# One weight load of the last feed-forward stage issued as fifteen loads of a few partitions each

## The chip, the cores and the metric

The kernel runs on one core of one Trainium2 chip. The metric is the device time of one execution in microseconds (us). Before the change it is 711.88 us, the median of three runs.

## The reference

Four tokens (B = 4, one per sequence) pass through an attention block and a feed-forward block, and then through both again with the same weights:

```python
x = A_x
x = x + _A_ref(_layernorm(x), A_k_cache, A_v_cache, A_wq, A_wo)   # 32 heads of 128, window 1024
x = x + _B_ref(_layernorm(x), B_w1, B_w2)                         # relu(x @ w1) @ w2
x = x + _A_ref(_layernorm(x), A_k_cache, A_v_cache, A_wq, A_wo)
x = x + _B_ref(_layernorm(x), B_w1, B_w2)
```

x is [4, 1, 640], w1 is [640, 1728], w2 is [1728, 640], all in float32. Per head the kernel needs a part of wq, the last 1024 keys and values of four sequences, and a part of wo. A head does not stay on the chip from the first round to the second, except for the last few.

## The kernel before

The host packs all that one head needs into one record of 9,472 float32 columns on 128 partitions (`rec`): wq, keys, values, wo. It packs w1 and w2 into a second array, `w`: first five pieces of 1,728 columns for w1 (one for each k, a fifth of the 640 inputs), then 54 tiles of 160 columns for w2. Two buffers on the chip take the loads: `slots`, five places of one record each, and `ring`, one place of 9,152 columns which the feed-forward stages use too.

The order of all loads is a list, `items`, written at the start. `pump()` takes loads from the head of the list and issues them on one queue, that of SyncE (SP), as long as the columns that a load will overwrite are free; `done()` and `free()` mark columns as free after the last use has been written down, and call `pump()`. Everything in that queue is issued in the order of the list, one instruction after the other, and an instruction that waits holds up all behind it.

The scheduling layer gives the loads eight completion semaphores in turn, DMAHW0 to DMAHW7. A load may not be issued before the load that used the same semaphore, eight loads earlier, has landed. So no more than eight loads are under way at a time, whatever their size.

The work around the change is the end of round two. After the record loads come the loads of the last feed-forward stage. The w1 loads are four, since the first two pieces travel together: 3,456 columns (k = 0 and 1), then 1,728 columns three times (k = 2, 3 and 4), all into `ring`. The w2 loads are five: 3,520, 2,240, 1,600, 640 and 640 columns, into a place of `slots`. On TensorE (PE), `mlp()` uses them in this order: 20 products with w1 in `h_ps`, relu and transposes, then products with the w2 tiles added into `acc`. Then VectorE copies the result to `scratch`, and SP issues the store of `out`. The constants `W1_SLOT` and `W2_SLOT` give the cuts of these loads.

Nearly all instructions are recorded by the helper `InOrder`, so the profile gives them its line 94 in the kernel before.

Of the kernel before, what the change touches and what calls it, by code (L numbers as in the profile page):

```python
# [2 lines left out]

# [11 lines left out]
P = 128  # L40
B, D, H, DH, W, FF = 4, 640, 32, 128, 1024, 1728
# [33 lines left out]
W1_SLOT = [[0, 1], [2], [3], [4]]  # L75
W2_SLOT = [22, 14, 10, 4, 4]
LATE = 5


class InOrder:  # L80
# [21 lines left out]
def decode_kernel(ctx: ExitStack, tc: tile.TileContext, xf, rec, w, out):  # L102
    nc = tc.nc
    pe, dve, act, pool, sp = (InOrder(tc, e) for e in (nc.tensor, nc.vector, nc.scalar, nc.gpsimd, nc.sync))
# [11 lines left out]
    hT = scratch.rearrange("p (m j) -> p m j", j=32)  # L116
    oTs = sb.tile([P, LATE, B], F32, name="oTs")
    qT = sb.tile([P, B], F32, name="qT")
# [59 lines left out]
    buffers = {"slots": slots, "ring": ring}  # L178
# [8 lines left out]
    def piece(r, h, lo, hi, buf=None, col=None):  # L187
        buf, col = place(home(h, r) if buf is None else buf, lo if col is None else col)
        items.append(([(("rec", r, h), lo, hi, col)], rec, h * REC + lo, h * REC + hi, buf, col))
# [9 lines left out]
    def ending(r, hs, late):  # L199
# [4 lines left out]
        if late:  # L204
            for h in hs[-1:] + hs[-LATE:-1]:
                piece(r, h, WO, REC)
# [8 lines left out]
    for h in hs[5 * NS:-3]:  # L215
        piece(0, h, 0, RING if h == SIXTH else WO if h >= H - LATE else REC)
    piece(0, SIXTH, RING, REC, "ring", 0)
    ending(0, hs, True)
    n = 0
# [22 lines left out]
    n = W1_COLS  # L242
# [4 lines left out]
    def pump():  # L247

        while items:
            parts, src, lo, hi, buf, col = items[0]  # L250
            if any(b == buf and x < col + hi - lo and col < y for b, x, y in live):
                return
            sp.dma_start(buffers[buf][:, col:col + hi - lo], src[:, lo:hi])
            live.append((buf, col, col + hi - lo))
            for key, x, y, c in parts:
                at.setdefault(key, []).append((x, y, buf, c))
            items.pop(0)
# [20 lines left out]
    def done(key, lo, hi):  # L278

        if key[0] == "rec" and key[1] == 0 and key[2] >= LAST:  # L280
            return
        if key == ("rec", 0, SIXTH):
            hi = min(hi, HELD)
        for x, y, buf, col in pieces(key):
            a, b = col + max(lo, x) - x, col + min(hi, y) - x
            if a < b:
                free(buf, a, b)
        pump()
# [5 lines left out]
    def put_by():  # L294

        for col, a, b in held:
            dve.tensor_copy(hold[:, col:col + b - a], ring[:, a:b])
            free("ring", a, b)
        free("ring", BESIDE, KEPT)
        pump()  # L300

    def lend():

        act.activation(*lent, AF.Copy)
        free("ring", HELD, BESIDE)
        pump()
# [193 lines left out]
    for r in range(2):  # L500
        hs = order[r]
        late = LATE if r == 0 else 2
        if r == 0:
# [92 lines left out]
```

## Time and profile before

| What | Value |
|---|---|
| device time, median of 3 runs | 711.88 us (711.86 to 713.6) |
| profiled execution | span 710.5 us from its first to its last instruction; its device time is not given beside it, and 711.88 less 710.5 leaves 1.4 us around a span |
| DMA | busy share 0.9 or more in 39 of 40 slices; mean 426 GB/s; 302.64 MB |
| PE busy | 513.6 us, 72% of the span |
| VectorE (DVE) busy | 323.3 us, 46% |
| ScalarE (ACT) busy | 99.7 us, 14% |

The profile gives an issue of a load as an instruction of SPq (about 0.33 us); the transfer itself goes on afterwards in 16 DMA engines, and its end is the landing. The views of windows give the busy share of those 16 engines in a stretch of time (the overlap of packets can bring it a little over 1.00) and the bytes moved.

### The profile page before, as it was taken

To read this page: it belongs to the slowest core of one execution; us is meant where nothing else is said; L and a number is where in the kernel's file an instruction comes from. 1 tells how busy PE (TensorE), PEld (TensorE's weight loads), DVE (VectorE), ACT (ScalarE), POOL (GpSimd) and SP (SyncE) were. 2 spreads that over 40 slices of the span, in tenths; PEclk is the share of its full clock that TensorE was granted. 3 is DMA by queue.
4 is the path that set the end of the run, shared out by engine and by line. 5 is a ranking of instruction groups with operands and counts; after the bars stand their busy time and mean duration, and the time that the engine had idled before them with its cause. 6 is when DMAs were issued, how large, how long until landed. Compare 5 with 4: busy or idle time off the path is not lost.

```text
span 710.5 us, 8690 instructions
## 1 busy us (share of the span) xinstructions
PE 513.6 (72%) x3706; PEld 202.8 (29%) x3706; DVE 323.3 (46%) x678; ACT 99.7 (14%) x211; POOL 1.1 (0%) x9
## 2 busy tenths in 40 slices
PE   3567686678584578857888898865686677576897
PEld 2132232232231223322223334331331322231423
DVE  3333353353452353546641777644352444253762
ACT  1100110011010110111121212201010111011111
POOL 0000000000000000000000000000000000000000
PEclk9957787677777776888999899977576677677899
DMA  9999999999999999999999999999999999999997
GB/s 381 463 409 451 415 442 443 414 442 444 424 429 440 434 429 421 435 425 430 424 416 403 421 435 428 438 434 448 429 445 427 428 442 430 427 442 406 431 423 292
DMA packets 13318, 302.64 MB, mean 426 GB/s; under 512 B 1488, under 2 KB 1760, under 8 KB 5216
## 3 DMA queue, kind: packets, MB, share of 16 engines
q1 hardware_dynamic: 13248, 302.08, 99.1%
q8 instruction: 29, 0.48, 0.2%
q14 instruction: 9, 0.07, 0.0%
q10 hardware_dynamic: 32, 0.01, 0.0%
HBM read 302.00 MB, written 0.08 MB: 425 GB/s over the span
## 4 chain that ended last, share of the span: by engine, by line
DMA 73%; PE 21%; DVE 4%; issue 1%; ACT 1%; SPq 0%; ACTq 0%; DVEq 0%
DMA slots<-rec 57%; PE sc_ps L94 11%; DMA ring<-w 8%; PE o_ps L94 7%; DMA ring<-rec 5%; PE acc L94 2%; DMA slots<-w 2%; DVE scratch L94 2%; DVE o_ps L94 1%; ACT oTs L94 1%; DVE small L94 0%; ACT sc_ps L94 0%; DVE turned L94 0%; SPq L94 0%; DVE ring L94 0%
## 5 line engine op out<-in xcount | busy, mean ns | idle before, releaser
L94 PE MATMUL sc_ps<-slots,qT 128*4 128x512 f32 x992 | 194.5, 869 | 37.4 <-DMA slots<-rec 36.4
L94 PE MATMUL sc_ps<-xT,slots 128*128 128x4 f32 x620 | 94.6, 279 | 99.8 <-DMA slots<-rec 99.2
L94 PE MATMUL o_ps<-slots,scratch 128*16 128x512 f32 x960 | 149.3, 693 | 2.4 <-DVE scratch L94 1.7
L94 DVE TENSOR_REDUCE small<-sc_ps 128x1 f32<-128x1024 f32 x64 | 78.3, 1224 | 156.9 <-PE sc_ps L94 156.9
L94 PEld LDWEIGHTS sc_ps<-xT,slots 128*128 128x128 f32 x620 | 89.2, 225 | 157.8 <-DMA slots<-rec 109.0
L94 ACT ACTIVATE sc_ps<-sc_ps,small 128x1024 f32<-128x1024 f32 (+1 forms) x68 | 71.1, 1046 | 342.2 <-DVE small L94 340.7
L94 DVE STREAM_TRANSPOSE turned<-sc_ps 128x1024 f32<-128x1024 f32 (+1 forms) x85 | 84.6, 996 | 0.7
L94 PEld LDWEIGHTS o_ps<-slots,scratch 128*16 128x16 f32 x960 | 34.5, 118 | 120.0 <-issue 107.6
L94 DVE TENSOR_TENSOR o_ps<-o_ps,of_block 128x512 f32<-128x512 f32 x62 | 43.4, 699 | 53.6 <-PE o_ps L94 52.3
L94 PEld LDWEIGHTS sc_ps<-slots,qT 128*4 128x4 f32 x992 | 32.3, 108 | 121.9 <-issue 64.9
L94 DVE TENSOR_TENSOR qT<-sc_ps,by_row 128x4 f32<-128x4 f32 x62 | 9.7, 156 | 114.1 <-PE sc_ps L94 114.1
L94 PE MATMUL acc<-slots,oTs 128*4 128x160 f32 x496 | 35.4, 368 | 19.2 <-ACT oTs L94 18.5
L94 DVE TENSOR_REDUCE scratch<-o_ps 128x128 f32<-128x512 f32 x62 | 42.9, 691 | 2.1
L94 ACT ACTIVATE oTs<-o_ps 128x4 f32<-128x4 f32 x64 | 11.1, 174 | 214.1 <-PE o_ps L94 214.1
L94 PE MATMUL o_ps<-pick,scratch 128*128 128x4 f32 x128 | 26.8, 280 | 15.9 <-DVE scratch L94 15.9
L94 PEld LDWEIGHTS o_ps<-pick,scratch 128*128 128x128 f32 x128 | 22.4, 218 | 21.4 <-DVE scratch L94 21.1
L94 DVE TENSOR_TENSOR scratch<-turned,by_row 128x128 f32<-128x128 f32 (+1 forms) x85 | 22.0, 259 | 3.2
L94 PE MATMUL sc_ps<-slots,small 128*1 128x512 f32 (+2 forms) x56 | 21.5, 486 | 0.0
L94 DVE TENSOR_SCALAR by_row<-of_batch,small 128x4 f32<-128x4 f32 x64 | 14.7, 230 | 2.2
L94 PEld LDWEIGHTS acc<-slots,oTs 128*4 128x4 f32 x496 | 6.9, 84 | 25.2 <-ACT oTs L94 23.5
L94 DVE STREAM_TRANSPOSE scratch<-small 128x32 f32<-128x32 f32 x64 | 12.9, 202 | 2.2 <-ACT sc_ps L94 2.2
L94 ACT ACTIVATION_READ_ACCUMULATOR sc_ps<-sc_ps,small 128x1 f32 x64 | 12.3, 193 | 0.0
(66 smaller groups left out, 103.7 us busy)
## 6 DMA issues: line engine op xcount, KB each, us to landing
slots<-rec SPq DMA_DIRECT2D x15, 7872.0 KB, 27.0
slots<-rec SPq DMA_DIRECT2D x8, 7936.0 KB, 31.5
slots<-rec SPq DMA_DIRECT2D x17, 2368.0 KB, 16.9
slots<-rec SPq DMA_DIRECT2D x4, 4736.0 KB, 25.9
slots<-rec SPq DMA_DIRECT2D x2, 4416.0 KB, 29.3
slots<-rec SPq DMA_DIRECT2D x7, 1024.0 KB, 19.7
ring<-w SPq DMA_DIRECT2D x8, 864.0 KB, 10.9
ring<-rec SPq DMA_DIRECT2D x1, 4576.0 KB, 36.2
```

Of the source, the lines that this page charges most:

```text
L94: r = build(*args, **kwargs)
```

## The change

The third w1 piece of round two, k = 2, columns 3,456 to 5,183 of `w`, is no longer one load of 128 partitions. It comes as fifteen loads, each of a band of neighbouring partitions: 2, 3, 4, and so on up to 15, and 9 at the end, 128 in sum. Destination, data and place in the list are the same. No other engine's instructions change. (Blank lines at the file's head are gone too, so that the same code has smaller line numbers: 94 becomes 72.)

```diff
+BANDED = 2 * FF
+BANDS = [2, 3, 4, 5, 6, 7, 8, 9, 10, 11, 12, 13, 14, 15, 9]
+assert sum(BANDS) == P
...
-            sp.dma_start(buffers[buf][:, col:col + hi - lo], src[:, lo:hi])
+            a = 0
+            for n in BANDS if parts and parts[0][:2] == (("w", 1), BANDED) else (P,):
+                sp.dma_start(buffers[buf][a:a + n, col:col + hi - lo], src[a:a + n, lo:hi])
+                a += n
```

SP's instructions from the first w1 load of round two on, before the change (partitions x columns, and the semaphores waited for):

```order
L94 DMA ring<-w 128x3456 [waits DMAHW6_49,DVE_49]
L94 DMA ring<-w 128x1728 [waits DMAHW7_49]
L94 DMA ring<-w 128x1728 [waits DMAHW0_49,DVE_49,Activation_49]
L94 DMA ring<-w 128x1728 [waits DMAHW1_49]
L94 DMA slots<-w 128x3520 [waits DMAHW2_49]
L94 DMA slots<-w 128x2240 [waits DMAHW3_49,PE_49]
L94 DMA slots<-w 128x1600 [waits DMAHW4_49,PE_49]
L94 DMA slots<-w 128x640 [waits DMAHW5_49,PE_49]
L94 DMA slots<-w 128x640 [waits DMAHW6_49,PE_49]
```

The first and the last of these nine rows wait for the same semaphore: the last w2 load waits for the landing of the 3,456-column load. The seven loads between them wait for record loads issued earlier.

The same place on SP after the change, first up to the seventh band:

```order
L72 DMA ring<-w 128x3456 [waits DMAHW6_49,DVE_49]
L72 DMA ring<-w 2x1728 [waits DMAHW7_49]
L72 DMA ring<-w 3x1728 [waits DMAHW0_49]
L72 DMA ring<-w 4x1728 [waits DMAHW1_49]
L72 DMA ring<-w 5x1728 [waits DMAHW2_49]
L72 DMA ring<-w 6x1728 [waits DMAHW3_49]
L72 DMA ring<-w 7x1728 [waits DMAHW4_49]
L72 DMA ring<-w 8x1728 [waits DMAHW5_49]
```

The seven waits for record loads are now those of the first seven bands.

And SP's next twelve instructions:

```order
L72 DMA ring<-w 9x1728 [waits DMAHW6_49]
L72 DMA ring<-w 10x1728 [waits DMAHW7_49]
L72 DMA ring<-w 11x1728 [waits DMAHW0_49]
L72 DMA ring<-w 12x1728 [waits DMAHW1_49]
L72 DMA ring<-w 13x1728 [waits DMAHW2_49]
L72 DMA ring<-w 14x1728 [waits DMAHW3_49]
L72 DMA ring<-w 15x1728 [waits DMAHW4_49]
L72 DMA ring<-w 9x1728 [waits DMAHW5_49]
L72 DMA ring<-w 128x1728 [waits DMAHW6_49,DVE_49,Activation_49]
L72 DMA ring<-w 128x1728 [waits DMAHW7_49]
L72 DMA slots<-w 128x3520 [waits DMAHW0_49]
L72 DMA slots<-w 128x2240 [waits DMAHW1_49,PE_49]
```

The eighth band (9 partitions) now has the wait for the 3,456-column load, which the last w2 load had; the fourth and fifth w1 pieces and all w2 loads stand behind it.

## The prediction

> **What bounds the kernel now.** I read the page first: the engines' shares, the slices, the chain that ended last. Then the chain in order of time, for the end of round two alone, since the change is there.
>
> ```profile
> span 710.5 us, 8690 instructions
> PE 513.6 (72%) x3706; PEld 202.8 (29%) x3706; DVE 323.3 (46%) x678; ACT 99.7 (14%) x211; POOL 1.1 (0%) x9
> DMA  9999999999999999999999999999999999999997
> DMA 73%; PE 21%; DVE 4%; issue 1%; ACT 1%; SPq 0%; ACTq 0%; DVEq 0%
> ...
> 660.59 0.33 SPq L94
> 661.02 29.53 DMA ring<-w
> 690.61 16.54 DMA slots<-w
> 707.19 0.50 PE acc L94 x8
> ```
>
> PE is busy 72% of the span, the DMA engines nine tenths or more in all slices but the last, and 73% of the chain is transfers. The chain's last rows (start, length, what) say how the end is made: the 3,456-column load is issued at 661.02 and lands 29.53 us later, just ahead of 690.61; at that moment SP issues the last w2 load, which lands 16.54 us after, at 707.15. Then only 0.5 us of PE and the store follow. So the kernel ends when the stream of loads ends, and what counts is whether the stream has a gap.
>
> Next, SP's issues one by one (start, length), from stretches that hold one each: the last two record loads shown first are the closest pair outside the kernel's start.
>
> ```profile
> 627.57 0.33 SPq L94 DMA_DIRECT2D slots<-rec  x1
> 627.95 0.42 SPq L94 DMA_DIRECT2D slots<-rec  x1
> 661.02 0.38 SPq L94 DMA_DIRECT2D ring<-w  x1
> 661.44 0.43 SPq L94 DMA_DIRECT2D ring<-w  x1
> 664.06 0.33 SPq L94 DMA_DIRECT2D ring<-w  x1
> 669.60 0.33 SPq L94 DMA_DIRECT2D ring<-w  x1
> 675.19 0.33 SPq L94 DMA_DIRECT2D slots<-w  x1
> 680.85 0.33 SPq L94 DMA_DIRECT2D slots<-w  x1
> 683.32 0.33 SPq L94 DMA_DIRECT2D slots<-w  x1
> 686.50 0.33 SPq L94 DMA_DIRECT2D slots<-w  x1
> 690.61 0.33 SPq L94 DMA_DIRECT2D slots<-w  x1
> ```
>
> From 661.44 on these are the nine loads of the order table less its first: three w1 loads, five w2 loads. Each is issued when one of the eight semaphores comes free, and each has a long backlog ahead of it: the fourth and fifth w1 pieces go out at 664.06 and 669.60, some 27 and 21 us before the 3,456-column load ahead of them has landed. That backlog hides every issue and every latency here.
>
> Third, the busy share of the 16 DMA engines at the end (the last three columns are granted clock, DMA share and GB/s).
>
> ```profile
> 702.00:703.00 1.00, 1.00 (x34) 0.92 (x28) 0.23 (x1) 0.00 (x0) 0.00 (x0) 1.00 1.00 412
> 703.00:704.00 1.00, 0.74 (x21) 0.33 (x17) 0.00 (x0) 0.00 (x0) 0.00 (x0) 1.00 0.75 306
> 704.00:705.00 1.00, 0.96 (x30) 0.50 (x21) 0.00 (x0) 0.00 (x0) 0.00 (x0) 1.00 0.62 250
> 705.00:706.00 1.00, 0.39 (x12) 0.32 (x16) 0.00 (x0) 0.00 (x0) 0.00 (x0) 1.00 0.44 167
> 706.00:707.00 1.00, 0.86 (x24) 0.31 (x12) 0.00 (x0) 0.00 (x0) 0.00 (x0) 1.00 0.10 38
> ```
>
> The share does not drop at once: 0.75, 0.62, 0.44, 0.10. The engines do not finish together. Some are through at 703, the last near 707, and the end waits for the last one. The mean engine ends 703 + 0.75 + 0.62 + 0.44 + 0.10 = 704.9, about 1.9 us ahead of the last.
>
> **The change part by part.** *Bytes and work.* The same 864 KB (885 KB in thousands) are moved; PE, DVE and ACT have the same instructions. Cost 0.
>
> *Bands one to seven (2 to 8 partitions).* They take over the waits and so the issue times of the seven loads that stood there, 661.44 to 686.50: all wait for landings that the change does not touch. Their transfers, 35 rows of 6,912 B, lie behind the 3,456-column load. Cost 0 by themselves, hidden by its backlog until 690.6. But they use up the places under way: where 6,912 - 320 = 6,592 KB of w1 and w2 stood in the queue at 690.6, there are now 35 rows, 236 KB, 0.6 us of the stream.
>
> *Band eight (9 partitions).* It waits for the 3,456-column load, so it goes out at 690.61. Here the cover is gone: behind it on SP stand seven more bands, the fourth and fifth w1 pieces and all of w2, and on PE the products of k = 3 and later wait for those.
>
> *Eight issues in a row.* Bands eight to fifteen and then the fourth w1 piece: it is issued eight intervals after 690.61. Their own semaphores do not hold them up: the ninth band waits for the first, the fifteenth for the seventh, which are queued behind the 3,456-column load and have at most 7 rows on one engine. One row takes 0.26 us on one engine (7,078 KB, the loads after the 3,456-column one, 6,912 x 1,024 B, in 16.54 us are 428 GB/s, 26.7 per engine; 6,912 B by that), so 7 x 0.26 = 1.8 us, through by 692.5, before the fifteenth's turn. The interval has no row for SP with so few partitions. Rows nearest to it:
>
> ```profile
> 1.23 1.53 SPq L94 DMA_DIRECT2D slots<-rec  x3
> ...
> 1.70 1.05 SPq L94 DMA_DIRECT2D slots<-rec  x2
> ...
> L94 ACTq DMA_DIRECT2D scratch<-xf x3: 256/318/645, 1.7 to 2.4; - x3
> q10 hardware_dynamic: 32, 0.01, 0.0%
> q1 hardware_dynamic: 13248, 302.08, 99.1%
> slots<-rec SPq DMA_DIRECT2D x1, 2368.0 KB, 8.3
> out<-scratch SPq DMA_DIRECT2D x1, 80.0 KB, 1.6
> ```
>
> Near the kernel's start one load follows another from 1.23 to 1.70, 0.47 us; the pair at 627.57 stands 0.38 apart, that at 661.02 0.42. ACT's loads of 4 partitions take 0.256 and 0.318 us before a last one of 0.645. So 0.30 to 0.47; I take 0.38, the pair on SP's own queue, since bands of 9 to 15 partitions lie between 4 and 128. Eight of them are 3.0 us: the fourth w1 piece goes out at 690.61 + 3.04 = 693.65.
>
> *Restart of an empty stream.* By then all engines but the lowest are idle, so the issue-to-landing overhead, so far hidden, is paid in the open once. Bounds: the store of 80 KB lands 1.6 us after its issue, of which 0.2 us is moving; 1.4 remain. The first load of the kernel, 2,368 KB, lands after 8.3 us, of which 2,425 KB at 428 GB/s are 5.7; 2.6 remain, on a cold queue and beside ACT's loads. I take 1.8, nearer to the store, since the queue is warm here, but a little over it, since a read has to fill from memory.
>
> *The rest of the stream.* From the fourth w1 piece on 6,048 KB remain, 6,193 KB in thousands, 14.47 us at 428 GB/s. All engines start them nearly together, so the spread at the end is gone, and this is in the sum already: the rate is that of the last engine.
>
> *Sum.* Last landing: 693.65 + 1.8 + 14.47 = 709.92, against 707.15 before: +2.8 us. The tail after it, 0.5 us of PE and the store, is the same. PE keeps up:
>
> ```profile
> 697.45 3.08 PE L94 MATMUL sc_ps<-ring,xT 128*4 128x432 f32 x32
> ...
> 701.53 1.90 PE L94 MATMUL acc<-slots,scratch 128*4 128x160 f32 x44
> ```
>
> it ends the w1 products at 697.45 + 3.08 = 700.5 and begins with w2 at 701.5; now the fifth w1 piece lands at about 693.65 + 1.8 + 4.1 = 699.6, and the first w2 load 4.2 us after that (1,802 KB in thousands at 428 GB/s), so PE waits for loads again and not they for it. Span 710.5 + 2.8 = 713.3. The span stands 1.4 us below the median of the runs, 711.88, and the difference is carried over to that: 714.7.
>
> Both ends: 8 x 0.30 with 1.4 gives 690.61 + 2.4 + 1.4 + 14.47 = 708.9, +1.7; 8 x 0.47 with 2.6 gives 690.61 + 3.76 + 2.6 + 14.47 = 711.4, +4.3. So 713.6 to 716.2.
>
> [...]
>
> **The rivals.** *A: the bands even out the engines, and the kernel gets faster.* Small loads need not use all engines. Page rows: q1 has 13,248 packets for 92 loads and stores, 144 each, that is 128 rows and 16 completions; q10 has 32 packets for four loads of 4 partitions, 8 each, 4 rows and 4 completions. So 4 rows went to four engines, one each. If n rows go to the same first n engines each time, the first gets 15 rows in place of 8 (+1.8 us), the ninth 8, the last none (-2.1 us). If the last engines are those that end near 707, and the first those that end at 703, the shares would be levelled and the stream could end up to 1.9 us earlier: 710.0. The falling shares above speak for it; against it, the trace doesn't say which engine is late, and the gain needs a stream without gap. It decides if the fourth w1 piece can be issued before the engines run dry, near 691; the wait of band eight excludes that, unless landings come some 3 us earlier. Chance 0.07.
>
> [...]
>
> *B: bands of odd size go to one engine.* 3, 5, 7, 9, 11, 13, 15 and 9 rows make 72 on the first engine, and each of the seven even bands adds one at least: 79 x 0.26 = 20.5 us in place of 2.1. The last landing would come near 690.5 + 20.5 + 14.5 = 725.5, 18.4 us later than now: 730. Against it: 4 rows went to four engines. Chance 0.03.
>
> *C: the gap is there, but short.* Intervals of 0.30 and a restart like the store's: +1.7, time 713.6, within 0.3%, which is 2.1 us and about what a measurement of this kernel can tell from no change. Chance 0.20.
>
> *D: a longer gap.* Each band lands on its own and the completions of one-row shares slow the low engines, so that band fifteen waits for the seventh: some 0.6 us on top of the high end, time 716.8. It is a share of the forecast's upper side, chance 0.12.
>
> **How the numbers follow.** The forecast's own band, a gap that costs 2.1 to 4.3 us, has 0.58; with D and B slower has 0.73. C gives same 0.20, A faster 0.07. The likeliest time is 714.7. The range takes in both bounds, 713.6 and 716.2, reaches up to D and down half a microsecond for an interval that is shorter still: 713.0 to 717.0; outside are A, B and a little of either side.
>
> **What would show it.** Band eight issued at 690.6 and the next 128-partition load near 693.7. A hole in the DMA share from about 691 to 695.5, with a few engines busy on single rows. A last landing near 709.9. A steep end: share near 1.00 until about a microsecond before that landing, in place of the ramp over 4 us. Packets on q1: 13,248 - 144 + 2 x 128 = 13,360 if each row has an engine of its own; fewer, if rows share one. The forecast is wrong if the share stays near 1.00 through 692 to 695 (then A), if issues of bands stand 0.6 us or more apart, or if the landing of the 3,456-column load itself moves.

## The result, and the profile after

The changed kernel takes 717.67 us (median of three runs, 717.34 to 718.03) against 711.88: 5.8 us more by the medians. The ratio taken over all runs, one of which took 713.6 before the change, is 1.0072 with a 95% interval of 1.0050 to 1.0094. The forecast was 714.7 with a range of 713.0 to 717.0: the direction was right, the size was too small by half. The profiled execution has a span of 716.0 us, 5.5 over that of before.

The page of the changed kernel, its head, its slices and its main queue:

```profile
span 716.0 us, 8708 instructions
PE 511.2 (71%) x3706; PEld 201.8 (28%) x3706; DVE 323.3 (45%) x678; ACT 99.7 (14%) x211; POOL 1.1 (0%) x9
DMA  9999999999999999999999999999999999999987
GB/s 384 465 395 451 443 417 436 439 435 430 432 443 426 421 447 428 429 420 428 423 409 413 420 427 436 434 454 422 441 437 416 443 445 413 439 442 406 426 267 326
q1 hardware_dynamic: 13360, 302.08, 98.8%
```

The computing engines do the same work. The last slice but one (680 to 698 us) has a DMA share of 0.8 but only 267 GB/s: the engines are busy and move little. The queue has 13,360 packets, the number that follows if each row of a band has an engine of its own.

The chain that ended last, in order of time (start, length, what), its end:

```profile
659.97 30.87 DMA ring<-w
690.85 0.27 SPq L72
691.17 0.32 SPq L72
691.53 0.33 SPq L72
691.90 0.34 SPq L72
692.29 0.36 SPq L72
692.70 0.37 SPq L72
693.11 4.47 DMA ring<-w
697.64 14.85 DMA slots<-w
712.53 0.50 PE acc L72 x8
```

Where two transfers stood, there is now a train of issues on SP between them. The 3,456-column load lands just ahead of 690.85, and the eighth band goes out at once. The transfer that begins at 693.11 is the band of 15 partitions; only when it has landed, 4.47 us after its issue, does the last w2 load go out. That load lands just ahead of 712.53, where PE starts; before, PE started there at 707.19.

Two more of SP's issues: that of the seventh band, which waits for the load ahead of the 3,456-column one, and that of the next 128-partition load, the fourth w1 piece:

```profile
686.34 0.27 SPq L72 DMA_DIRECT2D ring<-w  x1
...
693.96 0.36 SPq L72 DMA_DIRECT2D ring<-w  x1
```

PE in the same stretch; each row uses one w1 piece (k = 2, 3 and 4; its four products stand there as 8 instructions), and the bracket gives the wait ahead of it:

```profile
698.68 0.91 PE L72 MATMUL sc_ps<-ring,xT 128*4 128x432 f32 x8 [1.93 <-DMA ring<-w]
700.13 0.91 PE L72 MATMUL sc_ps<-ring,xT 128*4 128x432 f32 x8 [0.55 <-DMA ring<-w]
702.20 0.91 PE L72 MATMUL sc_ps<-ring,xT 128*4 128x432 f32 x8 [1.16 <-DMA ring<-w]
```

PE's start at 700.13, after a wait, dates the landing of the fourth w1 piece: 6.2 us after its issue, of which 2.1 are moving.

The DMA engines by windows (last three columns: clock, share, GB/s):

```profile
688.00:689.00 1.00, 1.00 (x10) 0.10 (x1) 0.91 (x2) 0.00 (x0) 0.00 (x0) 1.00 0.58 201
...
690.00:691.00 1.00, 0.52 (x9) 0.18 (x10) 0.88 (x3) 0.00 (x0) 0.00 (x0) 1.00 0.20 65
691.00:692.00 1.00, 0.74 (x11) 0.46 (x12) 0.00 (x0) 0.67 (x2) 0.00 (x0) 1.00 0.24 69
692.00:693.00 1.00, 0.96 (x5) 0.40 (x4) 0.70 (x3) 0.78 (x1) 0.00 (x0) 0.83 0.75 194
693.00:694.00 1.00, 1.00 (x9) 0.29 (x8) 0.42 (x3) 0.00 (x0) 0.00 (x0) 0.50 0.79 166
694.00:695.00 1.00, 1.00 (x7) 0.00 (x0) 0.00 (x0) 0.00 (x0) 0.00 (x0) 0.50 0.96 138
695.00:696.00 1.00, 1.00 (x7) 0.61 (x10) 0.00 (x0) 0.22 (x1) 0.00 (x0) 0.50 0.99 152
696.00:697.00 1.00, 0.75 (x8) 0.00 (x0) 0.50 (x3) 0.04 (x1) 0.00 (x0) 0.96 0.96 145
697.00:698.00 1.00, 0.00 (x0) 0.00 (x0) 0.00 (x0) 0.00 (x0) 0.00 (x0) 1.00 0.84 214
698.00:699.00 1.00, 0.32 (x4) 0.14 (x8) 0.00 (x0) 0.00 (x0) 0.00 (x0) 1.00 0.99 415
...
710.00:711.00 1.00, 0.31 (x14) 0.01 (x3) 0.00 (x0) 0.00 (x0) 0.00 (x0) 1.00 0.99 397
711.00:712.00 1.00, 1.00 (x28) 0.61 (x28) 0.00 (x0) 0.00 (x0) 0.00 (x0) 1.00 0.71 272
712.00:713.00 1.00, 0.70 (x16) 0.11 (x8) 0.00 (x0) 0.00 (x0) 0.00 (x0) 1.00 0.01 5
```

And before the change, at the place where the gap is now:

```profile
690.00:691.00 1.00, 1.00 (x12) 0.29 (x8) 0.90 (x3) 0.00 (x0) 0.00 (x0) 1.00 1.04 435
```

There is a gap, as forecast: a share of 0.20 from 690 to 691, where it was 1.04. It opens earlier than forecast, at 688 (0.58), since little but 35 rows stands behind the 3,456-column load. And its second half isn't idle: from 694 to 697 the share is 0.96 to 0.99 and the rate 138 to 152 GB/s, a third of what the same share gives at 698. Packets are under way, but few bytes arrive. The end is steep now (0.99, 0.71, 0.01, in place of a ramp over four windows), so the engines finish within about a microsecond of each other.

### The profile page after: what moved, and what is told of

It is laid out like the page before. It is cut to its first block, busy times and chain, and to the rows that moved or that the text cites. A ratio compares the mean times of both kernels' runs of the same rounds, so it can differ in the third digit from the quotient of the medians.

```text
span 716.0 us, 8708 instructions
## 1 busy us (share of the span) xinstructions
PE 511.2 (71%) x3706; PEld 201.8 (28%) x3706; DVE 323.3 (45%) x678; ACT 99.7 (14%) x211; POOL 1.1 (0%) x9
## 3 DMA queue, kind: packets, MB, share of 16 engines
q1 hardware_dynamic: 13360, 302.08, 98.8%
## 4 chain that ended last, share of the span: by engine, by line
DMA 71%; PE 21%; DVE 4%; issue 1%; another core or an unknown queue 1%; ACT 1%; SPq 0%; ACTq 0%; DVEq 0%
DMA slots<-rec 61%; PE sc_ps L72 12%; DMA ring<-w 8%; PE o_ps L72 8%; PE acc L72 2%; DMA slots<-w 2%; DVE scratch L72 2%; DVE o_ps L72 2%; ACT oTs L72 1%; SPq L72 0%; DVE turned L72 0%; DVE ring L72 0%; ACTq L72 0%; SPq L69 0%
## 5 line engine op out<-in xcount | busy, mean ns | idle before, releaser
L72 PE MATMUL sc_ps<-xT,slots 128*128 128x4 f32 x620 | 92.5, 276 | 100.8 <-DMA slots<-rec 100.1
L72 PE MATMUL o_ps<-slots,scratch 128*16 128x512 f32 x960 | 147.5, 681 | 1.1 <-DVE scratch L72 1.1
L72 PEld LDWEIGHTS sc_ps<-xT,slots 128*128 128x128 f32 x620 | 87.1, 220 | 157.7 <-DMA slots<-rec 109.0
L72 PE MATMUL sc_ps<-ring,xT 128*4 128x432 f32 x80 | 10.5, 573 | 4.8 <-DMA ring<-w 4.8
```

The costliest lines, as they stand in the source:

```text
L72: r = build(*args, **kwargs)
```

## The experiments

The question left by the trace: how much of the gap is the restart of an empty stream, and what slows the packets of the bands? In all runs only the k = 2 piece is cut in another way, and the eighth load behind the 3,456-column one is the one that waits for its landing. Each time is set against the kernel before on the same chip: 712.0 us (first four runs), 711.89 (next four), 711.77 (next three) and 711.89 (last three).

**Fifteen pieces by columns.** The same number of loads and waits, but each load on all partitions.

```diff
-BANDS = [2, 3, 4, 5, 6, 7, 8, 9, 10, 11, 12, 13, 14, 15, 9]
+PIECES = [116] * 12 + [112] * 3
...
-                sp.dma_start(buffers[buf][a:a + n, col:col + hi - lo], src[a:a + n, lo:hi])
+                sp.dma_start(buffers[buf][:, col + a:col + a + n], src[:, lo + a:lo + a + n])
```

> The k = 2 piece comes as fifteen loads again, but cut by columns (twelve of 116 and three of 112), each on all 128 partitions; number of loads, semaphores and waits as in the changed kernel. Theory (crowding: the fifteen loads drain the queue, and on top of that rows of neighbouring partitions under way together slow each other to a third of the usual rate): here only the drain is left, so the next 128-partition load goes out near 694.0 and lands some 4 us later, time +3 to +3.5 us over before. Rival 1 (restart: an empty stream takes about 4 us to come back whatever was in it): landing 6 us after the issue, time +5.5. Rival 2 (no drain, only crowding): +0.5 at most.

Measured: 717.66 us, ratio 1.0076 (1.0061 to 1.0091), as slow as the changed kernel. That fits the rival's number, but the trace shows that it is not for the rival's reason. SP's issues and PE's product with the fourth w1 piece:

```profile
685.93 0.33 SPq L72 DMA_DIRECT2D ring<-w  x1
...
690.07 0.33 SPq L72 DMA_DIRECT2D ring<-w  x1
...
694.98 0.36 SPq L72 DMA_DIRECT2D ring<-w  x1
...
699.76 0.91 PE L72 MATMUL sc_ps<-ring,xT 128*4 128x432 f32 x8 [2.32 <-DMA ring<-w]
```

The eight issues take 4.9 us, in place of 3.1; one of them alone takes 1.58, and no view shows what held it. The landing then comes 4.8 us after the issue, not 6.2: less 2.1 of moving, the restart is 2.7 us. And the 3,456-column load is on time, 4.14 us after the seventh piece (before: 690.61 - 686.50 = 4.11). So fifteen small loads cost as much in both forms, by another sum.

**Neighbours or rows spread out.** Twelve loads of 11 and 10 partitions, neighbouring, or 12 apart.

```diff
-BANDS = [2, 3, 4, 5, 6, 7, 8, 9, 10, 11, 12, 13, 14, 15, 9]
+BANDS = [11] * 8 + [10] * 4                       # neighbours
...
+STEP = 12                                         # spread, in place of the loop over bands
...
+            for a in range(step):
+                sp.dma_start(buffers[buf][a::step, col:col + hi - lo], src[a::step, lo:hi])
```

> Twelve loads of 11 (eight times) and 10 (four times) neighbouring partitions in place of fifteen bands. To be compared with the spread form of the same sizes. Crowding: rate falls to 100 to 150 GB/s while bands are under way, time +3 to +4.5 us over before. Restart: the next load goes out five intervals after the eighth band, near 692.6, landing 6 us later, +4. Uneven engines (low engines have 12 rows where the high ones have none): like the spread form.

> The same twelve loads by size, but load a takes the partitions a, a + 12, a + 24 and so on, so no two of its rows are neighbours. Crowding: the rate stays near 400 GB/s as far as engines have rows, time +1.5 to +2 us over before, 1.5 us or more below the form with neighbours. Restart: +4, like the form with neighbours. Uneven engines: the same as the form with neighbours.

Measured: neighbours 718.17 us, 1.0077 (1.0060 to 1.0094); spread 719.1 us, 1.0093 (1.0078 to 1.0108). The theory of neighbours expected the spread form 1.5 us or more below the other; it is not below. In the spread form an issue takes 0.74 us and the fourth w1 piece goes out 3.9 us after the eighth load; it lands 4.6 us after that (restart 2.5), with the DMA share at only 0.18 to 0.37 from 692 to 696. In both forms the 3,456-column load is late: 6.7 and 5.6 us after the seventh issue.

**The order of the bands reversed.**

```diff
-BANDS = [2, 3, 4, 5, 6, 7, 8, 9, 10, 11, 12, 13, 14, 15, 9]
+BANDS = [9, 15, 14, 13, 12, 11, 10, 9, 8, 7, 6, 5, 4, 3, 2]
```

> The same fifteen bands in the order 9, 15, 14, ..., 2: the first seven hold 84 rows and the eight late ones 44, where the changed kernel has 35 and 93. Crowding: less is left for the gap, but more disturbs the end of the 3,456-column load (its landing 0.5 to 1 us later); together +3.0 to +4.2 us over before. Restart: the issue comes about 0.5 us earlier than in the changed kernel since small bands are quicker to issue, +5.0.

Measured: 717.22 us, 1.0077 (1.0057 to 1.0097), +5.2 us, near the 5.0 of the rival, but not by its sum, which counts no delay of the 3,456-column load and keeps the landing some 6 us after the issue. In the profiled execution, span 715.1, the 3,456-column load lands 1.4 us late, and the fourth w1 piece 5.0 us after its issue (restart 2.9). With 84 rows ahead of the gap the load ahead of it is 1.4 us late, with 35 in the changed kernel 0.4; with 44 rows in the gap the piece behind lands 5.0 us after its issue, with 93 it took 6.2: the rows cost wherever they stand.

**Another source, the same destination; and each side alone.** The piece is read from an array of its own: for the bands, with rows 6,912 B apart; for the twelve loads, with the rows in another order, so that one side is neighbours and the other 12 apart.

```diff
+    arrays["wp"] = arrays["w"][:, BANDED:BANDED + FF]                                  # first run
...
+                    sp.dma_start(buffers[buf][r:r + n, col:col + hi - lo], wp[a::12, lo:hi])     # second run
...
+                    sp.dma_start(buffers[buf][a::12, col:col + hi - lo], wp[r:r + n, lo:hi])     # third run
```

> The changed kernel's fifteen bands, with the k = 2 piece read from an array of its own in which the rows follow each other without a gap (6,912 B apart instead of 69,120 B); the destination is the same. If rows of neighbouring partitions slow each other where they are read (memory), the next 128-partition load lands 4.6 us after its issue in place of 6.1, time +3.5 to +4.2 us over before. If they do where they are written, or at neither end, nothing changes: 6.1 us, time +5.2 to +5.8.

> Twelve loads of 11 and 10 rows, written to neighbouring partitions, read from rows that lie 12 apart (the rows stand in that order in a second array of the same pitch). Crowding where rows are written: as in the form with neighbours on both sides, the 128-partition load lands 6.5 us after its issue. Crowding where they are read: 4.6 us, as in the spread form. Time +5 to +7 us in both cases, since what the issues cost may differ.

> The mirror of the last: read from neighbouring rows, written to partitions 12 apart. Crowding where rows are written: the 128-partition load lands 4.6 us after its issue. Crowding where they are read: 6.5 us. It also tells which side makes an issue of spread rows cost 0.74 us in place of 0.29.

Measured: own array 717.93 us, 1.0082 (1.0067 to 1.0097); to neighbours 717.39, 1.0073 (1.0058 to 1.0088); from neighbours 719.12, 1.0100 (1.0085 to 1.0115). In the first the distance of the rows in memory makes nothing better: the fourth w1 piece lands 6.5 us after its issue, against 6.2 in the changed kernel. The other two are not conclusive: the landing comes 5.1 us after the issue for writes to neighbours and 4.5 for reads from them, but where rows are written 12 apart each issue takes 0.74 us again (0.29 where they are only read 12 apart), so the loads are never as dense, and the 3,456-column load is late in both, 5.3 and 6.4 us after the seventh issue.

**Fewer pieces by columns.** Eight and four in place of fifteen.

```diff
-PIECES = [116] * 12 + [112] * 3
+PIECES = [216] * 8      # and [432] * 4
```

> Eight column pieces of 216, all on 128 partitions, in place of fifteen. The eighth waits for the 3,456-column load as the eighth band does, but only one more issue stands between it and the next w1 piece. If the gap is made by the waits and by the issues behind them, the w1 piece goes out 0.45 us after the eighth piece, lands 4.7 us later: time +0.8 to +1.4 us over before. If it is the mere number of small loads that costs (0.36 us each, as fourteen more cost 5.1 in the fifteen pieces), +2.5.

> Four column pieces of 432 in place of fifteen. Now the load that waits for the 3,456-column one is the second w2 load, and two w1 pieces and a w2 load (3,488 KB, 8.3 us of the stream) are in the queue at that moment. If the gap comes from the queue running dry, nothing is lost: within 0.3 us of before. If each small load costs by itself, three more cost 0.5 to 1 us.

Measured: eight pieces 714.03 us, 1.0028 (1.0018 to 1.0037), +2.1 us; four pieces 712.2 us, 1.0002 (0.9993 to 1.0012), no difference. The DMA engines just at the landing of the 3,456-column load, with eight pieces and then with four:

```profile
690.00:691.00 1.00, 1.00 (x12) 0.30 (x8) 0.86 (x4) 0.00 (x0) 0.00 (x0) 1.00 0.45 152
```

```profile
690.00:691.00 1.00, 0.91 (x9) 0.25 (x10) 0.86 (x3) 0.00 (x0) 0.00 (x0) 1.00 1.05 425
```

Four pieces leave 3,488 KB of later loads queued behind the 3,456-column load, and the stream goes on. With eight, only the eighth piece's issue stands between the wait and the next w1 piece, and the stream runs dry already. The cost is more than the 0.8 to 1.4 us expected. In the profiled execution (1.6 us over before) the w1 piece lands 4.5 us after its issue, as expected, but what remains then takes 13.7 us in place of 12.4: from 707 on the share is 0.13 and 0.03, so one or two engines end later than the others. The rival by number of loads would fit eight pieces alone, but not four.

**Sixteen partitions per load.** Eight loads, in each of which, by the author's estimate, every engine has one row and none has more than another (in the changed kernel each row of a band has its own engine, by 13,360 packets); neighbours, and 8 apart.

```diff
-BANDS = [2, 3, 4, 5, 6, 7, 8, 9, 10, 11, 12, 13, 14, 15, 9]
+BANDS = [16] * 8        # spread: a::8 for a in range(8)
```

> Eight loads of 16 neighbouring partitions: as many loads and waits as the eight column pieces (+2.1 us), and one row per engine and load, so no engine has more than another. What is over that is crowding. [...] If the uneven engines made the changed kernel's excess, there is none: +2.1.

> Eight loads of 16 partitions that lie 8 apart, the rest as in the form with 16 neighbours. An issue of spread rows is slow (0.74 us), but only two stand behind the wait, some 0.8 us more. Crowding by neighbours: little of it here, +2.5 to +4 us, clearly below the form with 16 neighbours. Crowding by few rows per load whatever their place: like the form with neighbours or above.

Measured: neighbours 717.04 us, 1.0059 (1.0040 to 1.0079); spread 716.32 us, 1.0060 (1.0039 to 1.0080). Loads, waits and bytes are those of the eight column pieces, which cost 2.1 us; here it is 4.6 to 5.3 by the medians (the five runs with neighbours lie between 715.15 and 718.11, and the profile is of the fastest). That is not by neighbours, since both forms have it, nor, by the estimate of one row per engine, by uneven engines; of the expectations, only "few rows per load whatever their place" is left, and the next runs try it. SP's seventh and eighth issue of the eight column pieces, of 16 neighbours, and of 16 spread:

```profile
685.95 0.33 SPq L72 DMA_DIRECT2D ring<-w  x1
...
690.10 0.33 SPq L72 DMA_DIRECT2D ring<-w  x1
```

```profile
685.94 0.31 SPq L72 DMA_DIRECT2D ring<-w  x1
...
692.61 0.31 SPq L72 DMA_DIRECT2D ring<-w  x1
```

```profile
685.86 0.49 SPq L71 DMA_DIRECT2D ring<-w  x1
...
692.62 0.49 SPq L71 DMA_DIRECT2D ring<-w  x1
```

The eighth waits for the 3,456-column load, the seventh for the load before it; so the difference is what the 3,456-column load takes behind another, 4.15 us with column pieces, 6.67 and 6.76 with rows. From 687 to 688, while it is landing, the share is 1.05 and the rate 406 GB/s with column pieces, 1.00 and 228 with 16 neighbours, 0.97 and 235 with 16 spread. So it looks as if the rows behind it slow it; through what, no run shows.

**Which partitions.** Eight loads of 8 rows and one of 64: rows 4 apart in the lower half, 8 neighbours in the lower half, rows 4 apart in the upper half. The first of two expectations is that it matters which partitions the rows lie in, the second, the rival, that few rows per load are slow wherever they lie. Both are put as the time from the seventh issue to the landing of the 3,456-column load (4.15 us with eight column pieces) and as the time of the kernel over before.

```diff
-BANDS = [2, 3, 4, 5, 6, 7, 8, 9, 10, 11, 12, 13, 14, 15, 9]
+BANDS = [slice(a, a + 29, 4) for a in (0, 1, 2, 3, 32, 33, 34, 35)] + [slice(64, 128)]            # 4 apart, lower half
+BANDS = [slice(a, a + 8) for a in range(0, 64, 8)] + [slice(64, 128)]                             # neighbours, lower half
+BANDS = [slice(64 + a, 64 + a + 29, 4) for a in (0, 1, 2, 3, 32, 33, 34, 35)] + [slice(0, 64)]    # 4 apart, upper half
```

> Eight loads of 8 partitions, 4 apart, from the lower half (0, 4, ... 28, then 1, 5, ... and so on, then 32, 36, ...), and one of the upper 64. [...] Rival (few rows per load are slow as such): 5.1 us or more. Time +2.5 to +3.5 us over before by the first, +3.5 to +4.5 by the second.

> The same nine loads by size, the first eight of 8 neighbouring partitions. [...] Rival (few rows per load): the same as with rows 4 apart.

> [...] Rival (few rows per load): no difference to the first of the three.

The seventh and eighth issue again, with the window from 687 to 688 between them: rows 4 apart in the lower half, neighbours in the lower half, and rows 4 apart in the upper half.

```profile
686.00 0.62 SPq L71 DMA_DIRECT2D ring<-w  x1
...
690.09 0.62 SPq L71 DMA_DIRECT2D ring<-w  x1
...
687.00:688.00 1.00, 1.00 (x12) 0.24 (x8) 0.90 (x3) 0.00 (x0) 0.00 (x0) 1.00 0.90 380
```

```profile
685.90 0.27 SPq L71 DMA_DIRECT2D ring<-w  x1
...
691.21 0.27 SPq L71 DMA_DIRECT2D ring<-w  x1
...
687.00:688.00 1.00, 0.88 (x10) 0.21 (x9) 0.86 (x3) 0.00 (x0) 0.00 (x0) 1.00 0.80 214
```

```profile
685.89 0.62 SPq L71 DMA_DIRECT2D ring<-w  x1
...
692.66 0.62 SPq L71 DMA_DIRECT2D ring<-w  x1
...
687.00:688.00 1.00, 0.76 (x8) 0.21 (x9) 0.56 (x3) 0.53 (x2) 0.00 (x0) 1.00 0.99 207
```

4 apart in the lower half: 4.09 us, no delay, and 380 GB/s at a share of 0.90; by the share that is the rate of before (435 at 1.04 from 690 to 691). Neighbours: 5.31 us, and 214 GB/s at a share of 0.80. 4 apart in the upper half, with the same strides and the same issues as the first: 6.77 us, and 207 GB/s at a share of 0.99. So few rows per load do not delay the load ahead as such; it depends on which partitions they lie in. That engines get in each other's way where they write was the author's theory; it is not shown, since the trace doesn't number the engines and no run tells which one writes where. The rows read change along with the partitions written, so these three runs alone do not exclude a cause where rows are read; the run with an array of its own speaks against it, and the two runs after that leave it open. The times are 716.4 us, 1.0058 (1.0043 to 1.0073); 716.59, 1.0064 (1.0047 to 1.0081); 718.25, 1.0085 (1.0070 to 1.0100). By its landing the first of the three runs goes against the rival (5.1 us or more), by its time it doesn't: 4.5 us over before, above the 2.5 to 3.5 of the first expectation and at the upper end of the rival's range. The loss lies after the wait, where three long issues take 2.6 us and the fourth w1 piece lands 6.3 us after its own; probably the last load, of 64 partitions, meets the same trouble (159 GB/s at a share of 0.88 from 692 to 693), but no run shows that.

In the changed kernel a share of 0.96 to 0.99 from 694 to 697 means that nearly all sixteen engines are busy, and at 138 to 152 GB/s slow, though no band has more than 15 rows; no run here takes that apart.

## Why the prediction was right or wrong

| Term | predicted | measured |
|---|---|---|
| 3,456-column load behind the one before | 4.11 us, no change | 690.85 - 686.34 = 4.51: +0.4 |
| eight issues from its landing on | 3.04 | 693.96 - 690.85 = 3.11 |
| restart, issue to landing less moving | 1.8 | 700.13 - 693.96 - 2.07 = 4.1 |
| rest of the stream after that landing (both dated by PE's starts) | 14.47 - 2.07 = 12.40 | 712.53 - 700.13 = 12.40 |
| sum, against 16.54 | +2.8 | 0.4 + 3.11 + 4.1 + 14.47 - 16.54 = +5.5 |

*Right.* The mechanism: the bands use up the eight places, the eighth waits for the 3,456-column load, and the stream runs dry behind it. Four column pieces against eight show that it is the queue running dry and not the number of loads. The interval of issues, the rest of the stream, the steep end and the packets were right; that the rest fits to the hundredth is luck, since with eight column pieces the same bytes took 13.7 us. Rivals A and B are out: 13,360 packets, each row on its own engine.

*The step that failed is the restart of an empty stream.* It was taken as 1.8 us between bounds of 1.4 and 2.6, and measured 4.1, outside both; that a load needs more than a store since it is read from memory was the author's estimate, which no run isolates. Two parts: alone it is 2.5 to 2.7 (fifteen column pieces; rows 12 apart), at the bound that the kernel's first load had given and that the text set aside as cold. The other 1.4 to 1.6 us are what is left of 4.1, and the late bands explain them: 93 rows, 643 KB in thousands, which the sum put at nothing ("by then all engines but the lowest are idle"). They move at 138 to 166 GB/s; the band of 15 lands at 697.6, PE waits for the last of k = 2 until 698.68, and the fourth w1 piece, queued behind them, comes at 700.13. With 44 late rows in place of 93 the restart was 2.9.

*A second step was wrong in kind:* "bands one to seven, cost 0" and "one row takes 0.26 us on one engine". The rate behind that figure, 26.7 GB/s per engine, holds with rows 4 apart in the lower half (380 GB/s at a share of 0.90, 26.4 per busy engine). With the same rows in the upper half it is 207 at 0.99, 13.1 per busy engine. And rows can make the load ahead of them late, by 0.4 us in the changed kernel, by up to 2.7 us in the experiments. That the landing of the 3,456-column load moves was one of the prediction's own signs of being wrong. Rival D named one-row loads that hold each other up, but put 0.6 us on them and looked for them in the semaphores.

*The theory held in the first experiments, neighbours, fell too*: spread rows were no better. What decides, by the last three runs, is which partitions the rows lie in (4.09, 5.31 and 6.77 us); why was not shown.

Open stay: how the 5.8 us split in the unprofiled runs; why the engines end unevenly again with eight column pieces; what holds single issues of SP for 1 to 2 us, as in the fifteen column pieces; and whether reading from neighbouring rows adds something of its own (with twelve loads the 3,456-column load lands 6.7 and 6.4 us after the seventh issue where they are read from neighbours, 5.6 and 5.3 where they are read 12 apart, whichever way they are written; the eight loads of 16 rows show no such difference).

## What to carry to other kernels

Before a load is cut into many, count the loads that may be under way: when the pieces fill the places, the next one waits for a big load to land, and the whole backlog that hid issues and latency is gone; the price is the issues behind that wait plus one restart (here 3.11 and 4.1 us). If it must be cut, few pieces by columns are cheaper than as many by partitions: eight cost 2.1 us by columns and 4.6 to 5.3 by partitions. Cutting by columns is no cure for the drained queue: with fifteen pieces both forms cost the same (717.66 and 717.67 us). And where the bytes per second are low while the DMA share is high, look at which partitions the loads under way have, not for idle engines: 8 rows 4 apart went with 380 GB/s at a share of 0.90 in the lower half and with 207 at 0.99 in the upper.

## What the runs showed of the hardware that was not expected

The DMA share is no measure of the rate: 0.99 went with 152 GB/s in the changed kernel and with 415 GB/s three microseconds later. An issue on SP depends on its partitions: 0.25 to 0.38 us for 3 to 15 neighbours, 0.33 to 0.43 for 128, but 0.62 where 8 written partitions are 4 apart and 0.74 where 11 are 12 apart; rows that are only read 12 apart cost 0.29. And the restart of a warm, empty stream took 2.5 to 2.7 us beyond the bytes, about as much as the 2.6 of the kernel's first load.
